# Windowed attention and a squared-ReLU layer on one core: batch 1's q and k and batch 0's last third loaded by casting DMAs, and a new order of the work

## The chip, the core and the metric

The kernel runs on one core of a Trainium2 chip. A core has five engines that work side by side, each in the order of its own queue: TensorE (PE, matmuls, with a weight load before each, PEld), VectorE (DVE), ScalarE (ACT), GpSimd (POOL) and SyncE (SP), which only issues DMAs here. They wait for one another and for DMAs by semaphores. DMAs issued by SP and ACT are hardware DMAs ("hardware_dynamic" in the profile); those issued by POOL are software DMAs ("software_dynamic") and can change the type of what they carry, fp32 to bf16.

The metric is the device time of one execution in microseconds (us). The kernel before takes 219.99 us, the median of three runs (219.75 to 220.44).

## What is computed

```python
def _attn_ref(q, k, v, n_sink, window):            # q, k, v: (4, 8, 768, 64) fp32; 4 sinks, window 128
    scores = scale * np.matmul(q, k.transpose(0, 1, 3, 2))
    is_sink = pos[None, :] < int(n_sink)
    in_window = (rel >= 0) & (rel < int(window))
    scores = np.where(is_sink | in_window, scores, -1000000000.0)
...
    a = a / (np.sum(a, axis=-1, keepdims=True) + 1e-09)
    return np.matmul(a, v)

def _moe_ref(x, w_in, w_out):                      # x: (3072, 512), w_in: (512, 2048), w_out: (2048, 512)
    r = np.maximum(x @ w_in, 0.0)
    return (r * r) @ w_out
```

The attention's result, with its eight heads side by side, is `x`, the input of the second function. The kernel computes in bf16 with fp32 sums and returns fp32.

## The kernel before

There are four batches of 768 rows. Each batch is cut into six tiles of 128 rows and three slices of 256 rows. The eight heads are four pairs. For each batch these stages follow one another, and the stages of several batches overlap:

- **prep.** q and k are needed with the head dimension on the partitions. Batches 0 and 1 load them as fp32 on SP's queue (`load_qk`, L400, tile `qr`), cast them to bf16 on DVE, ACT or POOL ("regroup", L249, L247, L250, tile `qs`), turn them on PE with matmuls against the identity (L533, tile `pt`) and copy the result out (tile `qkT`). Batches 0 and 1 do so in two groups, four tiles and then two (`GROUPS`). Batches 2 and 3 (`NATURAL`) load q and k by casting DMAs on POOL's queue (`load_natural`, L432, tile `qn`) and turn them by DMA on SP's queue (L488), so that PE, DVE and ACT have no part in it.
- **scores and masks.** Each query sees at most 128 keys back and four sinks. Scores (L634, tile `ps`) go through an exponential on ACT (L654, tile `expm`). The window's mask is a multiplication on DVE (L663, L666) or a selection on POOL (L273). In batch 0, slices below `BIASED` = 2 have the mask added into the scores by matmuls (L627) instead. Sinks have their own small scores (L593).
- **values.** L704 multiplies with `v`, which POOL's queue loads cast to bf16 (`load_v`, L413); DVE divides by the sum (L720, L721) into `xn`.
- **bridge.** `xn` is turned into `xT`: by PE (L753, tile `px`) and a copy for batches 0 and 1, by DMA on SP's queue (L735) for batches 2 and 3.
- **layer 1.** L781 multiplies `xT` with `w_in`, in units of 1024 result columns (four weight blocks of 256 columns, or two of 512), here called tiles; ACT takes the maximum with 0 (L792, tile `r`) and DVE squares (L799, tile `gT`).
- **layer 2.** Batch 0's first two slices multiply with `w_out` directly (L819, 64 matmuls of 512 columns). All others use a fast scheme of seven products for eight (L927), which needs four weight sums, formed once on DVE (`weight_sums`, L860, from all four quarters of `w_out`), and four sums of `gT` per slice (L888). Results are copied and added (L247, L249, L948, L964, L971) and stored from SP's queue (L842, L996). The very last slice has its own ending (`tail`: L989, L990, L1001, L1002).

The order on each engine is not written by hand. Every piece of work is an `op` with a key, the engines it may run on with a cost for each, and what it comes after. `Plan.run` walks through them with these costs and, among those that can run, takes the one with the earliest start and then the lowest key, and records its instructions. `PLACES` shifts and scales the keys of each group. So costs and keys only decide the order and the engine; on the chip each engine runs its queue in that order and waits where it has to.

Loads on one queue are chained, so they are issued in the order in which the kernel's last part lists them. `behind` makes a load wait until a load of the other queue has landed. POOL's order before: four v loads, the four quarters of `w_in`, two quarters of `w_out`; then, behind SP's q and k of batch 0's last third, the third quarter of `w_out`, two v, the fourth quarter, then v of batch 1, then the loads of batches 2 and 3. SP's q and k of batch 0's last third wait for the first quarter of `w_out`, and batch 1's wait for batch 0's last v. Eight DMAs of a queue can be under way: each has one of eight semaphores, and a ninth waits until the first has landed.

PE warms up with idle matmuls (`warm`, L242) where the plan sees a gap in the first 34 us.

Of the kernel before, what the change touches and what calls it, by code (L numbers as in the profile page):

```python
# [11 lines left out]
FP32 = mybir.dt.float32  # L12
BF16 = mybir.dt.bfloat16
# [3 lines left out]
LATENCY = 0.145  # L17
PE_SLACK = 0.0
DMA_START = {"sp": 1.2, "act": 1.2, "pool": 1.6}
# [3 lines left out]
    ('att', 0, 0): (-0.11, 0.89), ('att', 0, 1): (0.01, 0.98), ('att', 1, 0): (0.12, 1.07),  # L23
    ('att', 1, 1): (0.355, 0.92), ('att', 1, 2): (0.49, 2.5), ('att', 2, 0): (-2.39, 0.95),
    ('att', 2, 1): (0.035, 1.12), ('att', 2, 2): (0.46, 0.33), ('att', 3, 0): (-0.055, 0.92),
    ('att', 3, 1): (-2.63, 1.54), ('ev', 0, 2): (0.975, 0.97), ('ev', 1, 0): (-0.05, 0.83),
    ('ev', 1, 1): (-0.045, 0.96), ('ev', 1, 2): (-0.68, 0.7), ('ev', 2, 0): (0.005, 0.81),
    ('ev', 2, 1): (-0.155, 1.05), ('ev', 2, 2): (-0.28, 0.94), ('ev', 3, 0): (0, 0.93), ('ev', 3, 1): (0.055, 1.07),
    ('ev', 3, 2): (-0.135, 1.25), ('l1', 0, 0): (0.56, 1.29), ('l1', 0, 1): (0, 0.93), ('l1', 0, 2): (0.53, 1.42),
    ('l1', 1, 0): (-0.03, 0.78), ('l1', 1, 2): (0.07, 1.04), ('l1', 2, 0): (0.025, 0.85),  # L30
    ('l1', 2, 2): (1.485, 2.48), ('l1', 3, 0): (-0.235, 0.98), ('l1', 3, 2): (-0.07, 0.8),
    ('l2', 0, 0): (-0.2, 0.95), ('l2', 0, 1): (0.88, 0.45), ('l2', 0, 2): (0.255, 0.66),
    ('l2', 1, 0): (0.025, 1.05), ('l2', 1, 1): (7.97, 0.38), ('l2', 1, 2): (-0.045, 1.01),
    ('l2', 2, 0): (0.69, 1.56), ('l2', 2, 1): (-0.065, 1), ('l2', 2, 2): (-0.035, 0.83), ('l2', 3, 0): (-0.105, 1),
    ('l2', 3, 1): (0, 0.98), ('l2', 3, 2): (0.105, 1.52), ('prep', 0, 0): (0.03, 1.17), ('prep', 0, 1): (-0.025, 1),
    ('prep', 1, 0): (-0.275, 1.32), ('prep', 1, 1): (-0.065, 1.17), ('prep', 2, 0): (-0.11, 1.24),
    ('prep', 3, 0): (-0.685, 0.97), ('sink', 0, 0): (0.13, 0.99), ('sink', 0, 1): (0.365, 0.39),
    ('sink', 1, 0): (0.52, 0.41), ('sink', 1, 1): (-0.795, 0.96), ('sink', 2, 0): (-0.025, 1.19),
    ('sink', 3, 0): (-0.16, 1.06), ('sum', 0, 2): (-2.075, 0.53), ('sum', 1, 0): (-0.485, 1.14),
    ('sum', 1, 1): (-0.83, 2.23), ('sum', 1, 2): (-0.185, 0.94), ('sum', 2, 0): (0.25, 1.23),  # L40
    ('sum', 2, 1): (0.175, 1.42), ('sum', 3, 0): (0.025, 1.24), ('sum', 3, 2): (0.005, 1),
    ('turn', 0, 0): (0.05, 0.82), ('turn', 0, 1): (-0.045, 0.89), ('turn', 0, 2): (-0.2, 0.81),
    ('turn', 1, 0): (0.35, 0.8), ('turn', 1, 1): (-0.07, 0.96), ('turn', 1, 2): (-0.2, 1.02),
    ('turn', 2, 0): (0.3, 1.13), ('turn', 2, 1): (0.05, 1.16), ('turn', 2, 2): (0, 1.03),
    ('turn', 3, 0): (-0.12, 1.29), ('turn', 3, 1): (0.155, 1.15), ('turn', 3, 2): (0.085, 1.02),
    ('val', 0, 0): (0.05, 0.74), ('val', 0, 1): (0, 1.01), ('val', 0, 2): (0.07, 1.03),
    ('val', 1, 0): (0.005, 1.13), ('val', 1, 1): (-0.025, 0.93), ('val', 1, 2): (-0.17, 0.85),
    ('val', 2, 0): (-1.035, 1.74), ('val', 2, 1): (-0.105, 1.04), ('val', 3, 0): (0.02, 1.24),
    ('val', 3, 1): (0.21, 2.5), ('val', 3, 2): (-0.04, 1.04), ('wt', 0): (-0.28, 1.2),
# [12 lines left out]
class Op:  # L62
    def __init__(self, key, engines, run, after, takes, reads, dma, follow):
        self.key, self.engines, self.run = key, engines, run
        self.after, self.takes, self.reads, self.dma = list(after), list(takes), list(reads), dma
        self.follow, self.yields, self.margin, self.group = list(follow), [], 0.0, None
        self.end = self.issued = self.engine = None


class Plan:  # L70
# [17 lines left out]
    def place(self, places):  # L88
# [4 lines left out]
        for o in self.ops:  # L93
            if o.group in places:
                shift, scale = places[o.group]
                o.key = first[o.group] + shift + (o.key - first[o.group]) * scale

    def run(self):
# [12 lines left out]
        while left:  # L111
            best = None
            for o in ready:
# [27 lines left out]
                cand = (round(pick[1], 2), o.key)  # L141
# [33 lines left out]
def kernel(  # L175
# [102 lines left out]
    def fill(e):  # L278
# [5 lines left out]
        for i in range(2):  # L284
            nc.vector.memset(kblk[i], 0.0)
            nc.vector.memset(vs_sb[i], 0.0)
            nc.vector.memset(v_sb[i][:, :, :, D:D + 1], 1.0)
# [28 lines left out]

    bias_slot = Slot("sg", 8)
    c_fill = op(-9, {"dve": 2.5}, fill, takes=[bias_slot])
    c_ident = op(-9, {"pool": 0.3}, build_ident)
    c_tri = op(-0.15, {"pool": 0.6}, build_triangles)  # L320
    c_bias = op(-8, {"pool": 1.3}, build_bias)
    c_sinks = op(-7, {"pool": 0.5}, build_head_rows)
# [7 lines left out]
    def dma_op(queue, name, run, us, behind=None, takes=(), yields=()):  # L330
# [7 lines left out]
        o = op(-5, {queue: (0.85 if queue == "pool" else 0.5) + (0.3 if behind else 0.0)}, go, dma=us, takes=takes,  # L338
# [9 lines left out]
    def load_w_in(i, behind=None, yields=()):  # L348
# [5 lines left out]
            3.1, behind, yields=yields)  # L354

    def load_w_out(i, behind=None, yields=()):
# [5 lines left out]
            2.6, behind, yields=yields)  # L362
# [749 lines left out]
```

The softmax here doesn't subtract the row's maximum and nothing guards it: scores larger than these inputs give would overflow.

## Time and profile before

The profile is of one execution. Its time as a run is 220.95 us; its span, from the first instruction to the last, is 219.2 us, at a granted TensorE clock of 1.000. A row of the profile names line, engine and operation, the tile written and the tiles read, how many, and the busy time.

| engine or row | busy us | count |
|---|---|---|
| L781 PE, layer 1 | 87.9 | 576 |
| L927 PE, fast layer 2 | 72.5 | 560 |
| L704 PE, values | 30.8 | 480 |
| L634 PE, scores | 26.1 | 256 |
| L819 PE, direct layer 2 | 15.8 | 64 |
| L533 PE, turning q and k | 8.3 | 96 |
| L627 PE, bias | 4.4 | 16 |
| L753 PE, bridge | 3.7 | 48 |
| L792 ACT, maximum | 49.3 | 48 |
| L654 ACT, exponential | 43.6 | 48 |
| L799 DVE, square | 32.8 | 48 |
| L249 DVE, casts `qs` | 7.9 | 17 |
| L249 DVE, copies `qkT` | 6.9 | 10 |
| L250 POOL, casts `qs` | 5.7 | 6 |
| software DMAs, packets | | 52,608 |

Busy times of PE's rows overlap at their ends, since matmuls are pipelined; the pace of PE is better read from the chain, where a stretch of equal matmuls has its length and count.

### The profile page before, as it was taken

To read this page: it belongs to the slowest core of one execution; us is meant where nothing else is said; L and a number is where in the kernel's file an instruction comes from. 1 tells how busy PE (TensorE), PEld (TensorE's weight loads), DVE (VectorE), ACT (ScalarE), POOL (GpSimd) and SP (SyncE) were. 2 spreads that over 40 slices of the span, in tenths; PEclk is the share of its full clock that TensorE was granted. 3 is DMA by queue.
4 is the path that set the end of the run, shared out by engine and by line. 5 is a ranking of instruction groups with operands and counts; after the bars stand their busy time and mean duration, and the time that the engine had idled before them with its cause. 6 is when DMAs were issued, how large, how long until landed. Compare 5 with 4: busy or idle time off the path is not lost.

```text
span 219.2 us, 5185 instructions
## 1 busy us (share of the span) xinstructions
PE 208.1 (95%) x2168; PEld 159.6 (73%) x2168; DVE 150.9 (69%) x291; ACT 116.1 (53%) x150; POOL 70.8 (32%) x98
## 2 busy tenths in 40 slices
PE   6999999999897999999999979999999999999992
PEld 6459986368775899555888855578889666798881
DVE  6667445546999977883997664678886734497732
ACT  2784535837787574866814444993261623662110
POOL 7970004046999998300795000000001000000000
PEclk9999999999999999999999999999999999999999
DMA  5999973989999999999599995300034202000222
GB/s 166 274 164 204 218 205 48 197 272 323 223 150 145 126 153 202 148 136 135 70 82 196 109 219 162 72 3 14 13 105 161 48 4 96 0 3 0 96 99 97
DMA packets 83048, 28.17 MB, mean 128 GB/s; under 512 B 70352, under 2 KB 80976, under 8 KB 83024
## 3 DMA queue, kind: packets, MB, share of 16 engines
q0 software_dynamic: 52608, 10.49, 63.2%
q1 hardware_dynamic: 30232, 17.27, 34.8%
q8 instruction: 17, 0.28, 0.5%
q10 hardware_dynamic: 184, 0.07, 0.1%
q14 instruction: 7, 0.06, 0.1%
HBM read 27.30 MB, written 6.29 MB: 153 GB/s over the span
## 4 chain that ended last, share of the span: by engine, by line
PE 75%; DMA 8%; DVE 7%; POOL 4%; issue 1%; SPq 1%; ACT 1%; POOLq 0%
PE pm L781 35%; PE py L927 22%; PE py L819 7%; PE po L704 5%; DMA w_in_sb<-in_moe_w_in_dram 4%; DMA xT<-xn_sb 4%; PE ps L634 3%; POOL v L413 2%; DVE wt L860 2%; DVE sg L888 1%; DVE expm L663 1%; PE pt L533 1%; DVE gT L799 1%; PE px L753 1%; PE ya L927 1%
## 5 line engine op out<-in xcount | busy, mean ns | idle before, releaser
L781 PE MATMUL pm<-xT,w_in_sb 128*128 128x256 bf16 (+1 forms) x576 | 87.9, 308 | 1.4 <-DMA xT<-xn_sb 1.3
L781 PEld LDWEIGHTS <-w_in_sb 128*128 128x128 bf16 x576 | 62.4, 114 | 20.6 <-issue 2.6
L792 ACT ACTIVATE r<-pm 128x1024 bf16<-128x1024 f32 x48 | 49.3, 1026 | 43.3 <-PE pm L781 39.7
L799 DVE TENSOR_TENSOR gT<-r 128x1024 bf16<-128x1024 bf16 x48 | 32.8, 689 | 27.9 <-ACT r L792 27.5
L654 ACT ACTIVATE expm<-ps 128x1024 bf16<-128x1024 f32 (+1 forms) x48 | 43.6, 955 | 10.5 <-PE ps L634 10.4
L927 PEld LDWEIGHTS <-gT 128*128 128x128 bf16 x320 | 30.8, 98 | 3.9 <-issue 0.2
L273 POOL TENSOR_SCALAR_AFFINE_SELECT expm<-expm 128x512 bf16<-128x512 bf16 x12 | 10.3, 884 | 59.3 <-ACT expm L654 59.3
L927 PEld LDWEIGHTS <-sg 128*128 128x128 bf16 x240 | 22.8, 98 | 4.9 <-issue 1.7
L927 PE MATMUL py<-wt,sg 128*128 128x256 bf16 x160 | 20.6, 273 | 0.5 <-DVE gT L888 0.5
L927 PE MATMUL py<-wt,gT 128*128 128x256 bf16 x160 | 20.7, 273 | 0.0
L704 PE MATMUL po<-v,expm 128*128 128x65 bf16 x352 | 17.9, 193 | 1.1 <-DVE expm L663 0.5
L704 PEld LDWEIGHTS <-expm 128*128 128x128 bf16 x352 | 16.7, 97 | 3.2 <-issue 0.9
L927 PE MATMUL py<-w_out_sb,gT 128*128 128x256 bf16 x144 | 18.7, 273 | 0.0
L666 DVE TENSOR_TENSOR expm<-expm,tri 128x1024 bf16<-128x1024 bf16 x22 | 15.3, 707 | 4.5 <-ACT expm L654 4.4
L721 DVE TENSOR_TENSOR xn_sb<-po,rc 128x512 bf16<-128x512 f32 (+1 forms) x28 | 17.2, 615 | 1.0
L819 PE MATMUL py<-w_out_sb,gT 128*128 128x512 bf16 x64 | 15.8, 380 | 0.2 <-ACT r L792 0.2
L634 PE MATMUL ps<-qkT 64*128 64x128 bf16 (+1 forms) x256 | 15.2, 238 | 0.6 <-ACT r L792 0.3
L634 PEld LDWEIGHTS <-qkT 64*128 64x128 bf16 x256 | 8.1, 94 | 9.9 <-issue 8.5
L247 ACT ACTIVATE osb<-py 128x256 f32<-128x256 f32 (+1 forms) x14 | 6.3, 451 | 14.8 <-PE py L927 9.7
L704 PE MATMUL po<-vs,es 128*128 128x65 bf16 x128 | 12.9, 193 | 0.0
L249 DVE CAST qs<-qr 128x512 bf16<-128x512 f32 x17 | 7.9, 462 | 6.2 <-DMA qr<-in_k_dram 3.6
L704 PEld LDWEIGHTS <-es 128*128 128x128 bf16 x128 | 11.7, 97 | 0.0
(71 smaller groups left out, 225.9 us busy)
## 6 DMA issues: line engine op xcount, KB each, us to landing
out_dram<-osb SPq DMA_DIRECT2D x11, 512.0 KB, 3.3
v<-in_v_dram POOLq DMA_DIRECT2D x24, 128.0 KB, 6.4
qr<-in_k_dram SPq DMA_DIRECT2D x8, 256.0 KB, 5.8
qr<-in_q_dram SPq DMA_DIRECT2D x8, 256.0 KB, 5.4
w_in_sb<-in_moe_w_in_dram POOLq DMA_DIRECT2D x4, 512.0 KB, 10.7
w_out_sb<-in_moe_w_out_dram POOLq DMA_DIRECT2D x4, 512.0 KB, 11.0
qn<-in_k_dram POOLq DMA_DIRECT2D x12, 128.0 KB, 6.8
qn<-in_q_dram POOLq DMA_DIRECT2D x12, 128.0 KB, 6.6
```

The lines of the kernel that those rows point to most:

```text
L249: return nc.vector.tensor_copy(out=dst, in_=src)
L273: nc.gpsimd.affine_select(out=e_tile, in_=e_tile, compare_op=ALU.is_ge, fill=fill, base=i - 1, pattern=[[0, n], [1 if i else -1, 128]], ch ...
L634: nc.tensor.matmul(ps[:, h2, o:o + w], lhsT=qkT_sb[r, m, 1, c, :], rhs=qkT_sb[r, m, 0, qb:qb + w // 128, :], start=(i == 0 and not biased) ...
L654: nc.scalar.activation(out=x[:, :, o:512], in_=bank_t["s", b, s, m][:, :, o:512], func=AF.Exp, scale=scale)
L666: nc.vector.tensor_mul(y, y, tri.rearrange("p (o a) c -> p o (a c)", o=1).to_broadcast([128, 4, 256]))
L704: touch(("po", b, s, m0), e, nc.tensor.matmul(pv[:, i, h2, :], lhsT=lhsT, rhs=rhs, start=(n_ == 0), stop=(n_ == len(mms) - 1)), j)
L721: touch(("po", b, s, m0), e, nc.vector.tensor_tensor(out=xn_sb[:, 2 * s:2 * s + 2, 128 * (m0 + j0):128 * (m0 + j0 + nj)].rearrange("p i (j ...
L781: nc.tensor.matmul(pm[:, i, :], lhsT=w_in_sb[:, fb // 4, kb, fb % 4:512:4], rhs=xT[:, c0 // 256:(c0 + cw) // 256, kb, :], start=(kb == 0), ...
L792: nc.scalar.activation(out=o, in_=h, func=AF.Relu)
L799: (nc.vector if e == "dve" else nc.gpsimd).tensor_mul(gT_sb[c0 // 512][:, fbs[0]:fbs[0] + n, c0 % 512:c0 % 512 + cw], r, r)
L819: touch((b, u), e, nc.tensor.matmul(pm[:, i, :], lhsT=gT_sb[t // 4][:, fb, 128 * (t % 4):128 * (t % 4) + 128], rhs=w_out_sb[:, fb, :], sta ...
L927: use(name, e, nc.tensor.matmul(y, lhsT=x[:, i, :], rhs=w_[:, i, :], start=first and i == 0, stop=i == HB - 1, skip_group_check=not first))
```

## The change

Batch 1 joins the batches that load q and k by casting DMAs and turn them by DMA (`NATURAL`). Of its three slices the first two keep the PE bridge (`BRIDGED`), and the third is turned by DMA. Batch 0's last third is loaded by casting DMAs too (`load_cast`), but still turned on PE, straight from `qn`. All these loads go on POOL's queue in the order listed, and no load waits for the other queue. `BIASED` falls from 2 to 1, so batch 0's second slice is masked after its exponential. Squares may also run on ACT. The fills at the start are split so that batch 1's part can come later. In the tail the last product is made in two halves of 128 columns, and the halves are copied and stored one by one, ahead of the two larger stores. The planner gets a further lag per group and per op (`NUDGES`, some 330 entries), and all its costs and keys are new.

```diff
-LATENCY = 0.145
+LATENCY = 0.336
 PE_SLACK = 0.0
-DMA_START = {"sp": 1.2, "act": 1.2, "pool": 1.6}
+DMA_START = {"sp": 1.45, "act": 1.2, "pool": 1.6}
...
+        for i, (shift, lag) in NUDGES.items():
+            self.ops[i].key += shift
+            self.ops[i].lag += lag
...
-                cand = (round(pick[1], 2), o.key)
+                cand = (round(pick[1] + o.lag, 2), o.key)
...
+    def load_cast(b, tiles):
+
+        for ti in (1, 0):
+            for t in tiles:
+                takes = []
+                if (b, ti) not in qn_slot:
+                    qn_slot[b, ti] = Slot("qr", NT if b else 2)
+                    takes = [qn_slot[b, ti]]
+
+                def run(e, t=t, ti=ti):
+                    if (b, ti) not in qn_t:
+                        qn_t[b, ti] = work["qr"].tile([128, NT, DM], BF16, name="qn", tag="qr")
+                    return [nc.gpsimd.dma_start(
+                        out=qn_t[b, ti][:, t, :].rearrange("p (h d) -> p h d", d=D),
+                        in_=(q, k)[ti][b, :, 128 * t:128 * t + 128, :].rearrange("h p d -> p h d"))]
+                dma_op("pool", ("qk", b, ti, t), run, 1.2 if b and tiles[0] else 0.9, None, takes)
...
+                casted = (b, g) == (0, 1)
+                for ti in () if casted else (1, 0):
...
-                        masked.append(op(at(fm + 0.03), {"pool": 1.3} if first else
-                                         {"pool": 1.3, "dve": 0.7} if s else {"dve": 0.58},
-                                         domask, after=[ex] if first else [ex, late["masks"]]))
+                        masked.append(op(at(fm + 0.03), {"pool": 1.25, "dve": 0.7} if s else {"dve": 0.58},
+                                         domask, after=[ex, c_tri if s else late["masks"]]))
...
-                if b in NATURAL or b == 1 and s in TURNED:
+                if b in NATURAL and not (b == 1 and s in BRIDGED):
...
+            if e == "act":
+                nc.scalar.activation(out=g, in_=r, func=AF.Square)
+            else:
+                nc.vector.tensor_mul(g, r, r)
+        ops["sq", b, fbs[0], c0, cw] = op(key, {"dve": 0.7, "act": 1.05}, square, reads=[rs],
...
-            copy("act", h, y[:, 128:256])
-            copy("dve", o[:, 0, 0:128], y[:, 0:128])
+            use("a", "dve", copy("dve", o[:, 0, 0:128], y[:, 0]), 0)
+            use("a", "act", copy("act", h, y[:, 1]), 1)
+            nc.sync.dma_start(out=rows(0, 0, 128), in_=o[:, 0, 0:128])
             nc.scalar.dma_start(out=rows(0, 128, 256), in_=h)
-            nc.sync.dma_start(out=rows(0, 0, 128), in_=o[:, 0, 0:128])
...
-    NATURAL, TURNED, BIASED = (2, 3), (), 2
+    NATURAL, BRIDGED, BIASED = (1, 2, 3), (0,1), 1
...
+    load_w_out(0)
+    load_w_out(1)
+    load_cast(0, (4, 5))
+    load_v(0, 2)
+    load_cast(1, (0, 1))
+    load_cast(1, (2, 3))
+    load_v(1, 0)
+    load_w_out(2)
+    load_w_out(3)
+    load_cast(1, (4, 5))
+    load_v(1, 1)
+    load_v(1, 2)
```

In the built program the order on the engines follows from this. PE has 2154 matmuls instead of 2168. Its layer-1 tiles of batch 0 take the quarters of `w_in` in the order first, third, fourth, and the second last. The matmuls of L819 come in two halves, 32 with the first two quarters of `w_out` and 32 with the last two; batch 1's first scores stand just ahead of the second half. On POOL one selection of batch 0's mask stands ahead of the second quarter of `w_out`. On SP the 12 transposes of batch 1 stand where its plain loads were, ahead of or between the two stores of L842. On DVE 34 squares and 4 maxima stand, on ACT 14 squares and 44 maxima.

## The prediction

> **What bounds the kernel now.** I read the page first, for engine totals and the 40 slices:
>
> ```profile
> PE 208.1 (95%) x2168; PEld 159.6 (73%) x2168; DVE 150.9 (69%) x291; ACT 116.1 (53%) x150; POOL 70.8 (32%) x98
> ...
> PE   6999999999897999999999979999999999999992
> PEld 6459986368775899555888855578889666798881
> DVE  6667445546999977883997664678886734497732
> ```
>
> PE is busy 95% of the span, so the end is set by PE's work plus the few places where PE stands. Second view: busy time in four stretches (us; busy and count of PE, PEld, DVE, ACT, POOL; clock; DMA; GB/s):
>
> ```profile
> 29.44:55.50 26.06, 25.82 (x246) 16.44 (x246) 14.61 (x26) 14.98 (x21) 9.54 (x14) 1.00 0.95 220
> 55.50:71.50 16.00, 13.58 (x174) 11.29 (x174) 15.82 (x24) 12.68 (x19) 16.00 (x19) 1.00 2.37 164
> 71.50:128.60 57.10, 55.44 (x634) 43.09 (x633) 45.25 (x90) 33.05 (x42) 30.14 (x35) 1.00 1.71 137
> 128.60:215.10 86.50, 86.45 (x796) 67.00 (x795) 56.64 (x102) 38.18 (x48) 1.47 (x2) 1.00 0.23 64
> ```
>
> From 55.5 to 71.5 DVE works 15.82 of 16.00 us: there DVE is the limit, and from 71.5 on PE is. The third view, the chain that ended last (start, us, what), agrees: PE after the w_in load, DVE from 56 to 70.6, PE to the end.
>
> ```profile
> 10.70 9.77 DMA w_in_sb<-in_moe_w_in_dram
> 20.47 0.05 issue
> 20.51 8.93 PE pm L781 x80
> ...
> 57.48 1.13 DVE wt L860
> ...
> 65.56 0.70 DVE sg L888
> ...
> 70.64 0.36 PE po L704 x6
> 71.00 0.55 PE ps L634 x12
> 71.55 0.98 PE py L927 x8
> ...
> 196.73 13.97 PE py L927 x128
> ```
>
> Its pieces give PE's pace: 13.97/128 = 0.109 us for a 256-column matmul, and in the same way 0.216 (512 columns), 0.056 (128), 0.030 (65), 0.55 for twelve score matmuls. Counting the matmuls that the program has from its first fast product (71.55) to the last, at these paces, gives 143.6 us; the trace took 215.09 - 71.55 = 143.5. So a count at these paces gives the time of a PE-bound stretch.
>
> Fourth, the loads: when the w_in and w_out quarters were issued and how long they took to land, and POOL's issue of small loads.
>
> ```profile
> L352 POOL DMA_DIRECT2D w_in_sb<-in_moe_w_in_dram x4: 780/786/800, 10.0 to 12.2; - x4
> DMA to landing us min/median/max: 8.0/10.7/13.5
> DMA to landing us min/median/max: 5.0/11.0/17.1
> 56.10 5.35 POOL L413 DMA_DIRECT2D v<-in_v_dram  x6
> 61.41 1.80 POOL L432 DMA_DIRECT2D qn<-in_k_dram  x2
> 80.27 10.73 SPq L488 DMA_TRANSPOSE qkT<-qn  x6
> ```
>
> The first w_in quarter lands at 10.0+8.0 = 18.0, the last at 12.2+13.5 = 25.7: 2.57 us each, one after another. The second w_out quarter (issued at 13.5, the slowest of the second landing line) lands at 30.6: 2.45 each. So POOL's queue is one stream from the first v load on. Small loads (128 KB) are issued at 5.35/6 = 0.89 us. Six transposes beside such loads took 10.73/6 = 1.79 us each.
>
> **The change, part by part.** PE: 48 of 96 turns (L533) go, 48 x 0.056 = 2.69 us; 8 of 48 bridge turns (L753), 0.45; 8 bias matmuls of 512 columns (L627), 1.73; sink scores 1.82 -> 1.57. The last product becomes 32 matmuls of 128 columns, 1.79 for 1.74. In all PE's needed work falls from 198.5 to 193.5. Warm-up matmuls rise from 48 to 86 (+2.1 us) but stand in the first 20 us, where PE waits for loads; uncovered they would cost those 2.1.
>
> DVE: 9 casts (9 x 0.46), 6 copies (6 x 0.69), 14 squares (14 x 0.69) go; 4 relus (no row on DVE; the fp32 512-column rows at 0.69 doubled bound them at 1.4, ACT's row at 1.03), 2 masks (0.71), 2 xT copies (0.42) and a store copy come: about -11 us. ACT: 6 unloads, 4 xT copies and 4 relus go, 14 squares at relu's 1.03 come: about +3. From 71.5 to the end ACT has 71.2 us busy in 143.6, so those lie beside PE; were they on the path they would cost up to 14 x 0.34 = 4.8.
>
> Loads: 1 MB + 3 MB of plain q and k on SP's queue become 16 casting loads on POOL's, each issued by POOL (16 x 0.92 = 14.7 us, in exchange for 6 casts, 5.7). The new order there is v, w_in, w_out 0 and 1, four for batch 0, two v, eight for batch 1, two v, and only then w_out 2 and 3. Before, w_out 2 and 3 were in by 45.1. This position decides the time. Batch 0's second slice gets one mask on POOL and three on DVE (0.71 each) for its bias matmuls; they fall before 25.0, where PE waits for w_in, and would cost up to 2.1 if it did not. Building the triangle (0.71) moves behind the third w_in issue, so the first v load is issued 0.7 earlier, and so the stream: w_in's last quarter at 25.0, w_out 1 at 29.9. POOL then also stands at one mask (it waits for ACT's exp, 16.8 before, plus 2 x 0.88) ahead of w_out 1's issue: about 18.6, well before w_out 0 is in at 27.4, so the queue covers it.
>
> Then come 16 small loads. Below: a quarter of a w_in load, 0.64 (their bytes). Above: 0.89, since from 56.1 to 68 POOL issued 14 at that pace without standing at a landing, although only eight may be under way. I take 0.89, the same form: 14.2. Eight of batch 1's 12 transposes share the engines before w_out 2 lands: from 0 (hidden) to 1.79-0.89 = 0.90. Between 92.2 and 101.2 seven loads landed and 4 to 5 transposes ran, (9.0-7x0.89)/4.5 = 0.6, which I take as the like mixture: 4.8. w_out 2 itself 2.45. It lands at 29.9+14.2+4.8+2.45 = 51.4 (ends: 42.6 and 53.8).
>
> PE gets there earlier. The third w_in tile waits for the last quarter (25.0), and between this and w_out 2's matmul stand 22.1 us by count (6 tiles 10.5, 32 L819 matmuls 6.9, attention of batch 0's last third 4.7): 47.1. So PE stands about 4 us at w_out 2, and all that PE lost before, the waits for w_in included, costs nothing. If w_out 2 landed before 47.1 the end would follow PE. Behind that wait in PE's queue stands everything, 19.0 us to the first fast product (32 L819 matmuls, 4 tiles, 44 score and 72 value matmuls and a turn of batch 1), then 140.3 to the end: 51.4+19.0+140.3 = 210.7.
>
> SP's queue: the two plain output stores (L842) now stand behind ten and twelve transposes, the last of which wait for batch 1's last q and k tiles, 53.9+4x0.89 = 57.5 and their issue, some 60; the two output buffers they free are wanted only after the first fast product near 70, which covers it by ten.
>
> What is late next is the DVE chain to that first product: w_out 3 lands 2.45 after w_out 2, at 53.9; then on DVE four weight sums (2x1.42+2x1.21), two masks 1.25, two triangles 1.4, four squares 2.8, a copy 0.7, two norms 1.8, xT copies 0.8, first sum 0.7: 14.7 -> 68.6, while PE arrives at 70.4. It is covered by 1.8 us; without the copies and casts taken out it would not be.
>
> Tail: before, from PE's last matmul (215.09) to the span's end 4.1. The first half is now copied while the second is multiplied (-0.45), but SP issues the two larger stores behind that half's store instead of ahead of it; three issues of 0.33 to 0.42, then a landing of 1.9 for the 256 KB store against 1.8: +0.2. Span 210.7+4.3 = 215.0. Before, the span 219.2 was 220.95 as a profiled run, and the median is 219.99, 0.8 over the span. So **215.8 us**.
>
> [...]
>
> **Rivals.** (1) Slower: the small loads and transposes starve w_out 2. Place: PE at L819's second half. Price: one us for each us of landing; from 56.2 on the kernel is slower. If all 16 went at the 1.79 of the mixed row it would be 29.9+28.6+2.45 = 61.0, and 225.4. For it: the mixed row, and before's 1.3 us wait for xT. Against: half of the 16 precede every transpose. (2) The DVE chain or masks set the first fast product again, at 71.6 as before: then only the later count is saved, 143.6-140.3 = 3.3, less 0.2 of tail, so 220.0-3.1 = 216.9; with w_out 3 two us later on top, 218.9. For it: DVE 15.82 of 16.00 and a cover of only 1.8. Against: 8 us less DVE work there. (3) Loads run by bytes, w_out 2 is never waited for: 47.1+19.0+140.3+4.3+0.8 = 211.5. (4) The new order makes PE stand elsewhere for about the gain, 4 us: no change. Before has no more than 1.3 us of such a wait after 75.
>
> **How the numbers follow.** Forecast (213.5 to 217) 0.46; rival 2 above 217, 0.18; rival 3, 0.10; rival 4, 0.09; rival 1, 0.17. Within 0.3% is 219.33 to 220.65, what a measurement can tell. Faster 0.74, same 0.09, slower 0.17. Range 211.5 to 220.8: rival 3's sum below; above, both upper costs (53.8, 218.2) and rival 4; outside stay most of rival 1 and little below.
>
> **What would show it.** Right: PE waits some 4 us for a w_out load near 47 to 51 and the first fast product starts near 70; POOL's queue has 16 x 1024 packets more (68,992); DVE no longer full from 55 to 71; after the first fast product PE has under 2 us of waits. Wrong: w_out 2 landing after 56; DVE idle nowhere between 54 and 70; PE standing at xT, at sums or at ACT's squares after 100.

## The result, and the profile after

The changed kernel takes 231.46 us (median of four runs, 229.98 to 233.34) where the kernel before took 220.04 beside it: the ratio is 1.0522, with a 95% interval of 1.0421 to 1.0623. It is slower by 11 us; the forecast was 215.8, faster by 4. The profiled execution took 229.98, its span is 228.3; it is the shortest of the four, so the trace holds 9.1 of the 11 us. Here and below, a ratio leaves out runs that lie more than 1.5% above the fastest of their kernel (one each of pe_busy, hold_mid and early_turns, whose profile is of that run), a median keeps them.

The page of the kernel after, with the busy times, PE's slices, its clock and the two large DMA queues:

```profile
PE 207.3 (91%) x2150; PEld 160.2 (70%) x2154; DVE 141.0 (62%) x270; ACT 119.7 (52%) x148; POOL 80.3 (35%) x112
...
PE   7897888970799999998999989999999999999992
...
PEclk9999999998599999999999999999999999999999
...
q0 software_dynamic: 69248, 12.59, 78.9%
q1 hardware_dynamic: 31512, 14.91, 38.7%
```

PE has as much to do as before by its busy time, but a hole in the tenth slice (51 to 57), and its clock drops there and in the eleventh. All else is near the picture that was forecast: DVE is down from 150.9 to 141.0, and from the twelfth slice on PE is full. What stands in the hole is in the view of PE's waits:

```profile
PE ps L739 <- DMA qkT<-qn: 8.2, 1, 8.2
PE pm L884 <- DMA w_in_sb<-in_moe_w_in_dram: 2.0, 2, 1.1
PE pm L884 <- ACT r L895: 1.9, 2, 1.1
...
PE pm L884 <- DVE u L1061: 0.8, 1, 0.8
```

One wait of 8.2 us: the first scores of batch 1 (L739) wait for a DMA transpose, `qkT` from `qn`. It is not the wait for `w_out` that the prediction put some matmuls later. The chain that ended last passes the same place (start, us, what):

```profile
28.89 8.37 DMA qn<-in_k_dram
...
41.39 16.89 DMA qkT<-qn
58.27 0.14 issue
58.41 0.82 PE ps L739 x8
59.23 4.11 PE py L925 x12
...
80.39 2.62 PE py L1036 x24
```

The transpose of q's second tile is issued at 41.39 and lands 16.89 us later. Then twelve matmuls of 512 columns take 4.11 us, where 12 x 0.216 = 2.59 is their pace. The busy times in short stretches (us; PE, PEld, DVE, ACT, POOL; clock; DMA engines' share; GB/s) show why:

```profile
50.00:53.00 3.00, 0.20 (x1) 0.00 (x0) 0.14 (x1) 0.00 (x0) 0.00 (x0) 1.00 1.72 115
53.00:56.00 3.00, 0.00 (x0) 0.00 (x0) 0.00 (x0) 0.00 (x0) 1.75 (x2) 0.87 2.03 32
56.00:58.40 2.40, 0.00 (x0) 0.02 (x1) 0.00 (x0) 0.00 (x0) 0.61 (x1) 0.50 1.85 81
...
60.00:62.00 2.00, 2.00 (x6) 0.75 (x5) 1.86 (x3) 0.52 (x1) 0.88 (x1) 0.50 2.07 151
62.00:64.00 2.00, 2.00 (x15) 0.84 (x15) 0.24 (x1) 0.35 (x1) 0.04 (x1) 0.99 1.63 155
```

From 50.2 to 58.4 no engine computes (POOL's busy time there is the issue of three loads). The DMA engines are busy all that time (a share of 1.7 to 2.0 counts packets that overlap on an engine), yet they move 32 GB/s in 53 to 56. And when PE goes on, the granted clock is 0.50 until 62.

The whole loss lies before PE's first fast product (L927 before, L1036 after). Its first matmul starts at 67.03 before and at 80.23 after, 13.2 us later; from there to PE's last matmul the kernel before takes 147.8 us (67.03 to 214.80) and the kernel after 143.7, which gives 4.1 back. 13.2 - 4.1 = 9.1 is the difference of the spans.

### The profile page after: what moved, and what is told of

Same layout as the page of the kernel before. It is cut to its first block, busy times and chain, and to the rows that moved or that the text cites. A ratio compares the mean times of both kernels' runs of the same rounds, so it can differ in the third digit from the quotient of the medians.

```text
span 228.3 us, 5136 instructions
## 1 busy us (share of the span) xinstructions
PE 207.3 (91%) x2150; PEld 160.2 (70%) x2154; DVE 141.0 (62%) x270; ACT 119.7 (52%) x148; POOL 80.3 (35%) x112
## 3 DMA queue, kind: packets, MB, share of 16 engines
q0 software_dynamic: 69248, 12.59, 78.9%
## 4 chain that ended last, share of the span: by engine, by line
PE 71%; DMA 18%; POOL 4%; DVE 2%; SPq 2%; issue 1%; ACT 1%; POOLq 0%; ACTq 0%
PE pm L884 31%; PE py L1036 26%; DMA qkT<-qn 7%; DMA w_out_sb<-in_moe_w_out_dram 7%; PE ps L739 4%; PE po L807 4%; PE py L925 4%; DMA qn<-in_k_dram 4%; SPq L587 2%; POOL v L512 2%; POOL w_in_sb L442 1%; POOL vs L680 1%; PE ya L1036 1%; DVE xn_sb L824 1%; ACT r L895 0%
## 5 line engine op out<-in xcount | busy, mean ns | idle before, releaser
L895 ACT ACTIVATE r<-pm 128x1024 bf16<-128x1024 f32 x44 | 45.1, 1025 | 52.4 <-PE pm L884 50.9
L906 DVE TENSOR_TENSOR gT<-r 128x1024 bf16<-128x1024 bf16 x34 | 23.5, 692 | 26.7 <-ACT r L895 26.5
L1036 PEld LDWEIGHTS <-gT 128*128 128x128 bf16 x336 | 31.5, 98 | 3.9 <-issue 0.3
L354 POOL TENSOR_SCALAR_AFFINE_SELECT expm<-expm 128x512 bf16<-128x512 bf16 x16 | 11.3, 730 | 51.3 <-DVE osb L1061 41.1
L1036 PEld LDWEIGHTS <-sg 128*128 128x128 bf16 x240 | 22.8, 98 | 3.2 <-issue 0.5
L739 PE MATMUL ps<-qkT 64*128 64x128 bf16 (+1 forms) x256 | 14.9, 241 | 8.9 <-DMA qkT<-qn 8.2
L771 DVE TENSOR_TENSOR expm<-expm,tri 128x1024 bf16<-128x1024 bf16 x24 | 16.8, 706 | 7.4 <-ACT expm L759 7.3
L1036 PE MATMUL py<-wt,gT 128*128 128x256 bf16 x160 | 20.7, 273 | 0.0
L1036 PE MATMUL py<-wt,sg 128*128 128x256 bf16 x160 | 20.6, 273 | 0.0
L739 PEld LDWEIGHTS <-qkT 64*128 64x128 bf16 x256 | 8.4, 95 | 17.1 <-issue 15.2
L1036 PE MATMUL py<-w_out_sb,gT 128*128 128x256 bf16 x144 | 18.7, 273 | 0.0
L512 POOL DMA_DIRECT2D v<-in_v_dram x12 | 10.8, 909 | 12.0 <-DMA v<-in_v_dram 7.0
L904 ACT ACTIVATE gT<-r 128x1024 bf16<-128x1024 bf16 x14 | 14.8, 1056 | 0.3
L768 DVE TENSOR_TENSOR expm<-expm,mask 128x768 bf16<-128x768 bf16 x12 | 6.6, 558 | 12.8 <-ACT expm L759 12.0
L531 POOL DMA_DIRECT2D qn<-in_q_dram x12 | 10.6, 890 | 6.3 <-DMA qn<-in_k_dram 5.1
## 6 DMA issues: line engine op xcount, KB each, us to landing
qn<-in_q_dram POOLq DMA_DIRECT2D x20, 128.0 KB, 12.1
```

What stands on the lines that cost most here:

```text
L512: return [nc.gpsimd.dma_start(out=v_sb[b % 2][:, t, :, 0:D], in_=v[b, :, 128 * t:128 * t + 128, :].rearrange("h p d -> p h d"))]
L739: nc.tensor.matmul(ps[:, h2, o:o + w], lhsT=qkT_sb[r, m, 1, c, :], rhs=qkT_sb[r, m, 0, qb:qb + w // 128, :], start=(i == 0 and not biased) ...
L771: nc.vector.tensor_mul(y, y, tri.rearrange("p (o a) c -> p o (a c)", o=1).to_broadcast([128, 4, 256]))
L895: nc.scalar.activation(out=o, in_=h, func=AF.Relu)
L904: nc.scalar.activation(out=g, in_=r, func=AF.Square)
L906: nc.vector.tensor_mul(g, r, r)
```

## The experiments

To move one load and nothing else, the order that the planner made (every instruction of every engine) was written down and replayed, and only the named loads change their place. All runs were timed beside the kernel before, and ratios are to it. That kernel took 220.04 beside the kernel after, 221.46 beside the next three of the table, 220.80 beside the early_turns and first two pe_turns kernels and 221.20 beside the other three, so rows are better compared by ratio than by median. "Turned" stands for a landed DMA transpose; tiles are batch 1's six token tiles.

| kernel | median us | ratio (95%) | first fast product | PE's waits for batch 1's turned tiles |
|---|---|---|---|---|
| after | 231.46 | 1.0522 (1.0421 to 1.0623) | 80.23 | 8.2 (tile 1) |
| wout_early | 226.05 | 1.0230 (1.0171 to 1.0290) | 76.22 | 4.7 (tile 1) |
| wout_small | 225.57 | 1.0224 (1.0168 to 1.0280) | 74.78 | 1.8 (tile 1), 1.9 (tiles 4, 5) |
| pe_busy | 230.95 | 1.0434 (1.0360 to 1.0508) | 79.95 | 1.4 (tile 1), 1.2 (tiles 2, 3), 0.3 (tiles 4, 5) |
| early_turns | 225.43 | 1.0161 (1.0101 to 1.0221) | 77.58 | 1.1 (tile 1), 4.6 (tiles 2, 3) |
| early_turns_small | 227.58 | 1.0243 (1.0210 to 1.0276) | 78.22 | 0.7 (tile 1), 6.1 (tiles 2, 3) |
| hold_mid | 230.02 | 1.0349 (1.0270 to 1.0428) | 80.90 | 3.2 (tile 1), 4.1 (tiles 4, 5) |
| hold_early | 228.25 | 1.0303 (1.0226 to 1.0379) | 80.27 | 1.6 (tile 1), 6.4 (tiles 4, 5) |
| pe_turns | 221.95 | 1.0055 (1.0024 to 1.0086) | 71.19 | 0.4 (tiles 4, 5) |
| pe_turns_early | 220.94 | 1.0015 (0.9983 to 1.0047) | 74.04 | none |
| pe_turns_mid | 220.11 | 0.9947 (0.9912 to 0.9983) | 71.61 | 0.7 (tiles 2, 3) |

In all eleven, PE needs 142.2 to 144.3 us from its first fast product to its last matmul. So the kernels differ by what happens before, and the experiments are about that.

### The disputed cost by itself: probe_dma

A kernel of DMA only, in eight stages, each behind all of the one before. It was run once.

```diff
+    stage("a", 4, [])                # four 128x512 transposes on SP's queue
+    stage("b", 0, big("b", 1))       # two w_out quarters on POOL's queue
+    stage("c", 0, big("c", 2))       # the same as halves of 256 columns
+    stage("d", 0, little("d"))       # eight 128 KB casting loads of k
+    stage("e", 4, big("e", 1))       # four transposes beside b's loads
+    stage("f", 4, big("f", 2))
+    stage("g", 4, little("g"))
+    stage("h", 4, [lambda i: w_in(f"win_h{i}", i)] * 2)
```

> This kernel computes nothing of the reference; it runs only DMA, in eight stages one behind the other: (a) four 128x512 transposes of batch 1's kind on SP's queue alone; (b) two w_out quarters on POOL's queue alone, as the changed kernel loads them (4096-byte packets); (c) the same two quarters as two halves of 256 columns each (512-byte packets); (d) eight casting 128-byte loads alone; (e) a's transposes beside b's loads; (f) beside c's; (g) beside d's; (h) beside two w_in quarters (1024-byte packets). Theory, an engine takes one packet from each queue in turn: 32 packets per engine of a transpose wait behind 322 ns each in stage e while w_out lasts (16 packets per engine, 5.2 us), so the first transposes land about 5 us later than in a, and in f and h only 1.5 to 3 us later (an estimate from 98 ns per 1024-byte packet); g no more than 1 to 2 us later. Rival, the engines share by bytes or time: e, f and h delay the first transpose alike, by some 1 to 2 us, since the bytes are the same.

The DMA issues of this kernel (tile written and read, queue, operation, count, KB, and the median time from issue to landing in us):

```profile
wout_b<-in_moe_w_out_dram POOLq DMA_DIRECT2D x2, 512.0 KB, 6.2
...
wout_e<-in_moe_w_out_dram POOLq DMA_DIRECT2D x2, 512.0 KB, 7.1
...
turn_a<-src SPq DMA_TRANSPOSE x4, 2.5
turn_e<-src SPq DMA_TRANSPOSE x4, 7.4
turn_f<-src SPq DMA_TRANSPOSE x4, 8.1
turn_g<-src SPq DMA_TRANSPOSE x4, 4.7
turn_h<-src SPq DMA_TRANSPOSE x4, 7.4
```

One by one, from the issues and the semaphores that the landings raise (us from issue to landing):

```
stage                        1st   2nd   3rd   4th transpose
a  alone                     2.5   2.5   2.5   2.5
e  beside 4096-byte packets  4.2   8.7   7.9   6.9
f  beside 512-byte packets   3.5   7.7   8.6   8.6
h  beside 1024-byte packets  4.0   7.6   8.3   7.3
g  beside 128-byte loads     2.5   4.2   5.2   6.6
```

A transpose alone lands in 2.5 us whatever its place. Beside casting loads it takes up to three and a half times as long (8.7). The loads lose less: from the first issue to the last landing they took 8.8 us in e (7.8 alone, in b), 11.8 in f (9.4 in c) and 12.1 in g (10.4 in d), so four transposes cost the loads 1.0 to 2.4 us, 0.3 to 0.6 each. The theory doesn't hold: the first transpose of e was 1.7 us late, not 5, and f was no better than e, so the size of the packets didn't decide when these four were through. The rival was right about the first transposes (1.7, 1.0 and 1.5 us late in e, f and h, where it had 1 to 2), but said nothing of the later ones, which were 4 to 6 us late, and in g the last was 4.1 us late where 1 to 2 at most were expected. In e and f they landed when the loads were done: in e the last at 48.21 with the loads in at 46.72, in f at 60.78 with 60.56. Small loads (stage d) went at 0.85 us each by themselves ((37.20 - 32.09) / 6 landings), so the price of 0.89 for them was right.

### The loads of w_out ahead of batch 1: wout_early

```diff
     load_v(0, 2)
+    load_w_out(2)
+    load_w_out(3)
     load_cast(1, (0, 1))
     load_cast(1, (2, 3))
     load_v(1, 0)
-    load_w_out(2)
-    load_w_out(3)
```

> The changed kernel with the order of every engine kept, except that the third and fourth w_out quarters are issued ahead of batch 1's first q and k loads instead of behind eight of them and two v loads. Theory (the transposes crawl because w_out's packets run beside them): the wait of PE for batch 1's second q tile, 8.2 us, shrinks to 0 to 2 us, the clock in 56 to 62 stays near 1.0, and the time is about 220 (219 to 222). Rival 1 (16 small casting loads and 8 transposes take that long in any order): the wait stays at 6 us or more and the time above 227. Rival 2 (other parts of the change cost the time after the first scores): the wait goes, the time stays above 225.

```profile
PE ps L938 <- DMA qkT<-qn: 4.7, 1, 4.7
```

Nearly half of the wait is gone and 5.4 us of the time (by the ratios 6.4), but not all: neither the theory (0 to 2) nor rival 1 (6 or more). `w_out` is in by 40.1, so nothing but casting loads of 128-byte packets stands beside the transposes now. They are still slow: the first was issued at 41.06 and landed at 48.30. The packet records of this run show no transpose packet until 44.0; until then POOL's loads start 1,208 packets of 128 bytes a microsecond (155 GB/s in 40 to 44).

### The same bytes in smaller packets: wout_small

```diff
-                out=w_out_sb[:, 4 * i:4 * i + 4, :],
-                in_=moe_w_out[512 * i:512 * i + 512, :].rearrange("(p f) m -> p f m", p=128))],
+                out=w_out_sb[:, 4 * i:4 * i + 4, c * w:c * w + w],
+                in_=moe_w_out[512 * i:512 * i + 512, c * w:c * w + w].rearrange("(p f) m -> p f m", p=128))
+                for w in ((256,) if i > 1 else (512,)) for c in range(512 // w)],
```

> The changed kernel with its order kept; the third and fourth w_out quarters are loaded as two halves of 256 columns each, so their packets are 512 bytes instead of 4096. Bytes, place in the queue and everything else are the same; POOL issues two loads more. Theory (one packet for one between the queues): transposes are held up by some 50 to 100 ns per packet instead of 322, the second q tile is turned by 51 to 54, PE waits 1 to 4 us instead of 8.2, time 222 to 227. Rival (bytes or the order of the loads alone count): the wait stays at 7 us or more and the time within 1 us of 230 to 232.

```profile
PE pk L898 <- DMA qkT<-qn: 1.9, 1, 1.9
...
PE ps L939 <- DMA qkT<-qn: 1.8, 1, 1.8
...
PE py L1125 <- DMA w_out_sb<-in_moe_w_out_dram: 0.8, 1, 0.8
```

Close to the theory: tile 1 is turned at 50.40 instead of 58.27, the wait is 1.8 and the time 225.57. So in this place of this order the 4096-byte packets do harm. A new wait appears behind it (1.9 us at L898, for the last two tiles).

### PE kept busy in the wait: pe_busy

```diff
                                 warm(ps[:, 0, 0:128])
+                                for _ in range(140 if (b, s, m0) == (1, 0, 0) else 0):
+                                    nc.tensor.matmul(ps[:, 0, 0:128], lhsT=ident, rhs=ident, start=True, stop=True)
```

> The changed kernel with 140 idle 128-column matmuls (140 x 0.056 = 7.8 us) put in PE's queue ahead of batch 1's first scores, where PE waits for the second q tile. The landings stay. Theory (the wait costs 8.2 us by itself and about 2 to 2.5 us more because TensorE's clock falls to 0.5 between 56 and 62 and the next matmuls run at half pace): clock near 1.0 there, twelve matmuls of L925 in about 2.6 instead of 4.11 us, and the time 1.5 to 2.5 us shorter than the changed kernel's. Rival (the fall of the clock is covered by later waits): no difference. Second rival (the clock fell for another reason than PE's idleness): the clock falls all the same.

PE's timeline there (start, us, what, and in brackets the idle time before it):

```profile
48.36 7.98 PE L927 MATMUL ps<-ident 128*128 128x128 bf16 x140
57.75 0.51 PE L940 MATMUL ps<-qkT 64*128 64x256 bf16 x8 [1.41 <-DMA qkT<-qn]
58.19 2.76 PE L1126 MATMUL py<-w_out_sb,gT 128*128 128x512 bf16 x12
...
65.24 0.62 PE L940 MATMUL ps<-qkT 64*128 64x128 bf16 x12 [1.15 <-DMA qkT<-qn]
```

The clock stays at 1.00 and the twelve matmuls take 2.76 (4.17 in the same view of the kernel after). So the clock fell because PE stood (0.50 in 56 to 58.4 of the kernel after, 1.00 here). But in the profiles the first fast product comes only 0.3 us earlier: what the clock gives, the next transposes take (1.15 us at 65.24) and a wait for POOL's masks (1.4 us in two) behind it. There the rival holds: the fall of the clock is covered. The times alone don't settle it: the medians are 230.95 and 231.46, the ratios 0.9% apart (1.9 us), and their intervals overlap.

### w_out behind the first four loads, in large and small packets: early_turns, early_turns_small

```diff
     load_cast(1, (0, 1))
+    load_w_out(2)
+    load_w_out(3)
     load_cast(1, (2, 3))
     load_v(1, 0)
-    load_w_out(2)
-    load_w_out(3)
```

> The changed kernel with every engine's order kept, but the third and fourth w_out quarters issued right behind batch 1's first four q and k loads (k0, k1, q0, q1), ahead of k2, k3, q2, q3 and two v loads. Packets stay 4096 bytes. Theory (engines go in step: each queue gets one packet in a turn, and a turn beside w_out lasts 0.33 us): the transposes now meet w_out from the start, 32 turns of 0.33 us for 32 of their 128 packets per engine, so the second q tile is turned at 51 to 55 and PE waits 2 to 6 us; time 223 to 228. Rival (less queued ahead, so the transposes are through first): second q tile turned before 49, no wait, time 219 to 221.

> The same order as early_turns, with the third and fourth w_out quarters loaded as halves of 256 columns (512-byte packets). Theory (turns of about 0.07 us): the second q tile is turned at 47 to 50, PE waits 0 to 2 us there, the clock holds, time 219 to 223, 3 us or more below early_turns. Rival (order decides, packet size does not): the same time as early_turns within 1 us.

PE's timeline of early_turns, then of early_turns_small:

```profile
51.18 0.51 PE L938 MATMUL ps<-qkT 64*128 64x256 bf16 x8 [1.09 <-DMA qkT<-qn]
...
62.07 0.62 PE L938 MATMUL ps<-qkT 64*128 64x128 bf16 x12 [4.55 <-DMA qkT<-qn]
```

```profile
50.63 0.51 PE L939 MATMUL ps<-qkT 64*128 64x256 bf16 x8 [0.65 <-DMA qkT<-qn]
...
63.03 1.03 PE L939 MATMUL ps<-qkT 64*128 64x128 bf16 x12 [6.07 <-DMA qkT<-qn]
```

The first wait is nearly gone in both, and tile 1 is turned at 51.05 and 50.50: the packets' size made no difference here, against the theory. (early_turns' time is in its range; early_turns_small took 227.58, which fits neither theory nor rival.) Both lose it again one pair of scores later, to the transposes of tiles 2 and 3, which are issued until 54.5 and land at 62 to 63. The wait moves; it doesn't go.

### POOL's queue held: hold_mid, hold_early

```diff
                 d = nc.gpsimd.dma_start(
                     out=v_sb[b % 2][:, t, :, 0:D],
                     in_=v[b, :, 128 * t:128 * t + 128, :].rearrange("h p d -> p h d"))
+                if (b, t) == (1, 0):
+                    for x in ((0, 2), (0, 3)):
+                        after_dma(d, loaded[("turn", 1) + x])
...
```

> The order of early_turns, and POOL's queue is held: the first v load of batch 1, and with it every casting load behind it, is issued only when the transposes of batch 1's tiles 0 to 3 have landed. No transpose is left out, none is turned elsewhere; the casting loads beside them are. Theory (a DMA transpose is slow only beside POOL's loads): the eight transposes land within about 3 us of each issue, the last by 54; the waits of 1.1 and 4.6 us that early_turns showed are at most 1 us together, first fast product at 70 to 73, time 219 to 222, unless the eight held loads, 5 to 8 us later than before, are waited for in their turn near 70. Rival (the transposes are slow by themselves, one behind the other): the waits stay at 4 us or more, time 224 or above.

> The same hold of POOL's queue with the order of wout_early: the third and fourth w_out quarters ahead of all of batch 1's q and k, then eight casting loads, then the hold. Theory: only the eight casting loads (until about 48) stand beside the first transposes; the wait of 4.7 us that wout_early showed shrinks to 0 to 2 us, time 219.5 to 222.5. Rival (the first transposes are held up by these eight loads alone): the wait stays at 3.5 us or more, time 223 or above.

In hold_early POOL's last load ahead of the hold lands at 49.30. The eight transposes took 6.7, 6.1, 6.7, 5.8, 5.1, 4.1, 2.5 and 2.5 us from issue to landing: those issued after 49.30 are as fast as alone. In hold_mid the loads end at 52.20, and the transposes issued behind that took 2.4 and 2.5, the four ahead of it that PE needs first 8.4 to 10.7. That part of the theory, slow only beside POOL's loads, holds. The times don't follow; both are above their ranges. For hold_early:

```profile
PE pk L901 <- DMA qkT<-qn: 6.4, 1, 6.4
...
PE ps L942 <- DMA qkT<-qn: 1.6, 1, 1.6
```

The wait for tile 1 is 1.6 (4.7 in wout_early), but the held loads are now issued from 55.5 on, the transposes of tiles 4 and 5 stand among the loads behind them until 76, and PE waits 6.4 us for these. It is the exception that the expectation of hold_mid named, and it costs more than the hold brings. hold_mid has the same wait (4.1 us), and one of 3.2 for tile 1, where at most 1 us was expected. Order alone, in whatever form tried here, only chooses which transpose PE waits for.

### Four of the twelve transposes taken off the DMA: pe_turns, pe_turns_early, pe_turns_mid

Tiles 0 and 1 of batch 1 are cast on load as in the changed kernel, but turned on PE (16 matmuls of 128 columns) and copied out by DVE and ACT.

```diff
-                                nc.sync.dma_start_transpose(
-                                    out=qkT_sb[:, :, ti, t, :], in_=qn_t[b, ti][:, t, :])
+                                if b > 1 or t > 1:
+                                    nc.sync.dma_start_transpose(
+                                        out=qkT_sb[:, :, ti, t, :], in_=qn_t[b, ti][:, t, :])
+                                    return
...
+                                for m in range(NP):
+                                    touch("pt1", e, nc.tensor.matmul(
+                                        pt[:, t, ti, m, :], lhsT=qn_t[b, ti][:, t, 128 * m:128 * m + 128], rhs=ident,
+                                        is_transpose=True, start=(ti == 1 and m == 0), stop=(ti == 0 and m == NP - 1)), t)
...
```

> The changed kernel with one part undone: the first two token tiles of batch 1's q and k are still cast on load, but TensorE turns them (16 matmuls of 128 columns, 0.9 us, ahead of the first w_out part of batch 0's first pair) and one copy each on VectorE and ScalarE takes them out; the other eight tiles are still turned by DMA. Theory (the wait for DMA transposes in the crowded stretch is what made the change slower): the 8.2 us wait is gone, four transposes less hold up w_out, PE waits at most 3 us for w_out, first fast product near 72 to 75, time 221 to 225 (a DMA transpose needed later may take part of it back). Rival (the casting loads alone crowd the queue): the wait moves to w_out and stays at 6 us or more, time 228 or above.

> pe_turns and the order of wout_early together: the third and fourth w_out quarters ahead of batch 1's q and k loads. Theory: both waits (for turned tiles and for w_out) are gone, PE goes on at 50 to 51, its first fast product starts at 70 to 72, and the kernel takes 217.5 to 220.5, the same as or a little less than the kernel before. Rival (the later transposes, tiles 2 to 5 of batch 1, then wait in PE's way): PE waits 3 us or more for qkT between 55 and 75 and the time stays above 222.

> pe_turns with the order of early_turns: TensorE turns batch 1's first two tiles, and the third and fourth w_out quarters are issued right behind these tiles' loads. Both are at hand when PE gets there (near 50); what is left are the eight DMA transposes of tiles 2 to 5. Theory: PE has no wait over 2 us between 45 and 75, time 219.5 to 222, between pe_turns and pe_turns_early. Rival: the transposes of tiles 2 and 3, now behind w_out, are waited for by 3 us or more before the second pair's scores, time above 223.

pe_turns has the changed kernel's order of loads, and takes 221.95: 9.5 us less (by the ratios 4.7% of before, 10.3 us), for one part undone, as its theory had it; the rival, that the loads alone crowd the queue, is out. Nothing was done to `w_out` there, and yet its third quarter lands at 46.50 and its fourth at 49.86, instead of 54.80 and 57.50. That is the prediction's sum without its term for transposes, 29.9 + 14.2 + 2.45 = 46.6 (of the four transposes that remain beside it, the first landed at 50.86). So the transposes and `w_out` had held each other up. Its view of waits also has one of 1.7 us for a transpose, but that is at 127.6, in layer 1 and far behind the stretch in question; the kernel before has one of 1.3 at 128.6.

In pe_turns_early no transpose of batch 1 is waited for; its profiled run lost 3.8 us to late `w_in` loads, before the stretch in question. Its first fast product (74.04 for 70 to 72) and its time (220.94 for 217.5 to 220.5) are above its theory's ranges. pe_turns_mid, with early_turns' order, is the best: ratio 0.9947, with an interval that excludes 1, so it is faster than the kernel before by half a per cent. PE's timeline of it:

```profile
45.84 1.05 PE L794 MATMUL pt<-ident,qn 128*128 128x128 bf16 x16 [0.40 <-DVE rc L1035]
...
50.72 0.50 PE L951 MATMUL ps<-qkT 64*128 64x256 bf16 x8
51.16 2.76 PE L1137 MATMUL py<-w_out_sb,gT 128*128 128x512 bf16 x12
...
57.79 0.62 PE L951 MATMUL ps<-qkT 64*128 64x128 bf16 x12 [0.74 <-DMA qkT<-qn]
```

The 16 turns take 1.05 us, the scores and `w_out`'s matmuls follow without a wait and at full clock, and the next tiles' transposes are waited for by 0.74.

## Why the prediction was wrong

The sum was: PE at `w_out` 2's matmul at 51.4, then 19.0, then 140.3, so PE's end at 210.7. Measured: 59.16, then 21.07 (to 80.23), then 143.91 (to 224.14). The three terms are off by 7.8, 2.1 and 3.6, together 13.4.

- **The step that failed** is the price of batch 1's transposes. The prediction costed them at 0.6 us each, and only as something that delays `w_out` 2; when they land themselves was not asked, though PE's scores stand ahead of `w_out` 2's matmul in its queue. 0.6 was a throughput read from a stretch where nothing waited for them; as what a transpose costs the loads beside it, probe_dma gives the like (0.3 to 0.6). What counts is issue to landing: 16.9 us for the one that PE needed, with `w_out` beside it (2.5 alone). pe_turns shows that this is the cause: without these four the wait goes and 9.5 us come back.
- **w_out 2**, 51.4 forecast, upper end 53.8, landed at 54.80, above both. Its semaphore goes up in 16 steps, and 15 of them were in by 48.38; the last came 6.4 us behind, while three large packets started in a microsecond (the table of packets below). PE did not wait for it, because the transpose was later still. The sign of being wrong that the prediction set here (after 56) therefore didn't show, and none of its signs looks at batch 1's turned tiles.
- **What stood ahead of it was right.** The last `w_in` quarter came at 25.97 (25.0 forecast), `w_out` 1 at 30.85 (29.9), the first v load of batch 1, fifteenth small load behind it, at 45.47; 30.85 + 15 x 0.89 = 44.2.
- **19.0 for the way to the first fast product** became 21.07: twelve matmuls at half clock cost 1.5 of it. By pe_busy this costs nothing here, since a later transpose would have been waited for instead.
- **140.3 to the end** became 143.9. The term was taken from a count that seemed to agree with the trace of before, 143.6 to 143.5. But the trace was measured from 71.55, the first row of L927 in the chain, and the count started with the program's first L927 matmul, which starts at 67.03. PE's timeline of before:

```profile
67.03 1.03 PE L927 MATMUL py<-wt,sg 128*128 128x256 bf16 x8 [0.52 <-DVE gT L888]
...
70.64 0.36 PE L704 MATMUL po<-v,expm 128*128 128x65 bf16 x6 [0.55 <-DVE expm L663]
...
71.48 1.05 PE L927 MATMUL py<-wt,sg 128*128 128x256 bf16 x8
```

  The chain had left PE for DVE between the two and so doesn't show the earlier one. At the same paces the matmuls from 71.48 on count to about 140.4, so the agreement of 143.6 with 143.5 was luck. From 67.03 to PE's end at 215.09 are 148.1 us for a count of 143.6: a counted stretch takes 3% more than the count. The same 3% on 140.3 is 144.7; 143.9 were measured. The saving forecast for this stretch, 3.3, is there, and a little more (4.1).
- **The tail** took 4.2 us (224.14 to 228.3), forecast 4.3. **DVE** is not on the path at the first fast product any more, as forecast: in 52 to 60 it works 0.15 of 8.00 us. **Squares on ACT** cost one wait of 0.8 us (at 105) after the first fast product; with one of 0.75 for DVE (at 136), 1.6 in all, forecast "under 2". POOL's queue has 69,248 packets, forecast 68,992.
- **The rivals.** Rival 1 had the place nearly right, the crowd of small loads and transposes between 31 and 58, and its sum at 1.79 us each, 225.4, was the only one on the right side; but it let `w_out` starve, and the transposes starved with it. It got 0.17, and "half of the 16 precede every transpose" was a bad argument against it: POOL issues ahead, in the kernel after up to eight of its loads are issued and not landed, and it is with these that a transpose has to share.

A number on the page of before pointed this way. Its DMA issues, and then those of the kernel after, give the transposes' median from issue to landing:

```profile
qkT<-qn SPq DMA_TRANSPOSE x24, 6.0
```

```profile
qkT<-qn SPq DMA_TRANSPOSE x36, 7.7
```

6.0 us, in stretches of casting loads that nothing waited for, ten times the 0.6 that the sum used. In the very stretch of before from which the prediction read 1.79 us a transpose (80 to 91), the view of DMA issues has:

```profile
qkT<-qn SPq DMA_TRANSPOSE x6, 8.4
```

So the number that failed could be read before the change: 1.79 was the distance from one issue to the next, 8.4 the time to landing.

What stays open: in the kernel after, the last of the 16 steps comes 6.4 us behind the 15th for `w_out` 2 and 5.7 for `w_out` 3. In pe_busy, which keeps that order, it is 4.9 and 5.5, in pe_turns 0.3 and 0.1. Why, the records don't tell. Nor is it settled why smaller packets helped in wout_small and not in early_turns_small or in the probe.

## What to carry to other kernels

Price a DMA by its issue-to-landing time beside what is queued with it, and compare that with the moment its reader gets there; a throughput says nothing of a deadline. A transpose moved from PE to the DMA engines was free here only where those had room: eight of batch 1's twelve were nearly hidden, and the four in the crowd cost 9.5 us against 1.05 us of PE and two copies. When a count is calibrated on a trace, take both from the same instruction.

## What the runs showed of the hardware

**Beside the last quarters of `w_out` transposes started some 50 packets a microsecond for 8 us, behind them 240.** Packets that started in each microsecond in the kernel after, from its packet records, by kind:

```
us        128-byte loads   4096-byte w_out   256-byte transposes
39-40          1146                0                 25
46-47             3               45                 47
47-48             3               43                 61
48-49             4               44                 50
53-54            50                3                 51
56-57            53                3                 56
58-59           734                0                240
```

In this trace a 4096-byte packet took 0.322 us (median), a 128-byte load's 0.032 and a transpose's 0.031; 16 / 0.322 = 50 of the large in a microsecond is the author's estimate for 16 engines. From 46 to 50 177 large packets started and 202 of the transposes, close to one for one. From 53 to 57 three large ones started in a microsecond (of the 16 steps of the semaphore of `w_out`'s last quarter, 15 are in by 51.83 and the last at 57.50), and the other kinds stayed at 37 to 64 each. In 58 to 59, with `w_out` in, they moved faster again: 734 and 240. pe_busy has the like of the slow stretch: 42 GB/s in 52 to 54 and 33 in 54 to 56, at a DMA share of 2.01 and 2.17. Why the small kinds were that slow, the traces don't show. A transpose alone landed 2.5 us after its issue in probe_dma, where eight casting loads of the same 128 KB, issued one behind the other, had a median of 4.4; beside loads a transpose took up to 16.9 (the kernel after).

**The granted clock fell and came back microseconds behind PE's stops and starts.** It fell 5.0 us after PE stopped in the kernel after (50.2 to 55.2) but 2.0 us after in wout_early (49.45 to 51.48), and came back 2.8 us (wout_small, 51.85 to 54.68) to 5.8 us (hold_mid, 52.3 to 58.1) after the work did. It was at 0.50 for 3.41 us in wout_small (51.27 to 54.68) and for 6.83, twice that, in the kernel after (55.23 to 62.06) and in wout_early (51.48 to 58.31); in the kernel after the full clock ahead of the fall lasted 47.79 (7.44 to 55.23), 14 times 3.41. The table has PE's busy share in stretches of 3.41 us that end at a change of the clock or 3.41 us ahead of one:

| stretch of 3.41 us | PE busy in it | clock in it | clock behind it |
|---|---|---|---|
| after, to 51.82 | 0.53 | 1.00 | 1.00 |
| hold_early, to 71.51 | 0.49 | 1.00 | 1.00 |
| wout_early, to 51.48 | 0.40 | 1.00 | 0.50 |
| wout_small, to 51.27 | 0.39 | 1.00 | 0.50 |
| after, to 55.23 | 0.00 | 1.00 | 0.50 |
| hold_mid, to 54.71 | 0.71 | 0.50 | 0.50 |
| wout_small, to 54.68 | 0.83 | 0.50 | 1.00 |
| after, to 62.06 | 1.00 | 0.50 | 1.00 |

In these rows the full clock was kept behind shares of 0.53 and 0.49 and lost behind 0.40, 0.39 and 0.00; the half clock stayed behind 0.71, and the full one came back behind 0.83 and 1.00. What else the clock goes by, they don't show.
